# Channels dealt by parity: weight rows with one stride over 128 rows, and mu in two transfers

## The chip, the cores and the metric

The kernel runs on one core of a Trainium2 chip. The metric is the device time of one execution in microseconds, the median of several runs. The names of the engines: PE is TensorE (matmuls; PEld are its weight loads), DVE is VectorE, ACT is ScalarE, POOL is GpSimd. SP (SyncE) computes nothing here: it is the queue from which all transfers are issued, in program order. The transfers themselves are moved by 16 DMA engines.

## The reference

Two parts, one after the other: causal attention in blocks of 64 positions for 8 batches and 8 heads, then a channel mix on its output. All inputs are float32.

```python
# attention: q, k, v are [8, 8, 576, 64]
scores = np.matmul(q, k.transpose(0, 1, 3, 2)) / np.sqrt(64)
scores = np.where(block_i >= block_j, scores, -1e9)      # blocks of 64 positions
attn = softmax(scores)
x = np.matmul(attn, v)             # then [8, 576, 512]: 512 channels = 8 heads x 64

# channel mix: mu_k, mu_r [512], w_k [512, 1024], w_v [1024, 512], w_r [512, 512]
x_prev = x shifted by one position (zero first)
xk = mu_k * x + (1 - mu_k) * x_prev
xr = mu_r * x + (1 - mu_r) * x_prev
k = np.maximum(xk @ w_k, 0)
out = sigmoid(xr @ w_r) * ((k * k) @ w_v)
```

## The kernel before

The attention output is produced with channels on partitions, since the channel mix contracts over channels. For one batch, the heads are handled in two groups of four (Q = 0, 1). The 64 columns of V of a head are cut in two halves of 32, x = 0 and 1. A matmul with a 128x32 weight block of V fills 32 partitions, and the four heads g of the group fill the four 32-partition strips next to each other:

```python
R = D // 2                                   # 32

def products(ps, lhs, a, z, last):
    for kc in range((z + P - 1) // P):
        q0 = max(a, kc * P)
        for g in range(G):                   # G = 4 heads side by side
            nc.tensor.matmul(
                ps[g * R:g * R + R, q0 - a:z - a], lhs(kc, g),
                probs(b, 4 * Q + g, kc, q0, z - q0), ...,
                tile_position=(0, g * R))

def part(i):
    ...
    for x in range(2):
        products(PS[:, x * w:x * w + w],
                 lambda kc, g: VOs[b % 2][:, kc, 4 * Q + g,
                                          x * R:x * R + R],
                 a, z, True)
```

So block cc = 2 * Q + x of the 512 channels (128 channels on 128 partitions) holds, on partition 32 * g + r, channel 256 * Q + 64 * g + 32 * x + r. The rows of w_k and w_r, and mu_k and mu_r, have to be loaded in the same order. The rows of w_v follow the hidden units and are plain:

```python
def add_w(name, n, ranks, rank):
    src = {"k": moe_w_k, "r": moe_w_r, "v": moe_w_v}[name]
    if name == "v":
        src = src.rearrange("(cc p) (n j) -> n cc p j", p=P, j=C)
    else:
        src = src.rearrange("(q g s r) (n j) -> n q s g r j", g=G, s=2,
                            r=D // 2, j=C)
    for i in range(n):                       # 8 blocks of w_k, 4 of w_r, 8 of w_v
        ld = plan.buf("ld")
        ...
        t = load(("w", name, i), lambda: new("ld", [P, S], FP),
                 lambda d, cc=cc, half=half: [
                     (d[:, 0:C], src[half, cc] if name == "v" else
                      src[half, cc // 2, cc % 2])],
                 ranks[i], 0.8, takes=[ld])
        ...                                  # then a cast to fp16, on DVE, ACT or POOL

def mus():
    for dst, src in ((MUK, moe_mu_k), (MUR, moe_mu_r)):
        src = src.rearrange("(q g s r o) -> q s g r o", g=G, s=2, r=D // 2, o=1)
        for cc in range(CCn):                # CCn = 4
            nc.sync.dma_start(dst[:, cc:cc + 1], src[cc // 2, cc % 2])
```

Each block of weights is 128 rows of 512 float32, 256 KB. It goes to a buffer of the ring `ld` (10 buffers, shared with the loads of q and k) and is cast from there.

All the work is given as tasks to a small planner in the kernel's own code. It puts the tasks of every engine into one fixed order, from ranks and from assumed durations (0.8 us for a block of weights). On the chip each engine runs its list strictly in that order: a cast that waits for its block holds back everything behind it on its engine.

The normalization of the attention output on DVE (line 690) reads the products from PSUM and writes `xt`; the mixes (lines 740 and 752) make `xk` and `xr` from it. The channel mix's matmuls are at lines 788 (w_k), 821 (w_r) and 850 (w_v). Line 624 has the sums of the softmax, line 609 the products with V, line 539 the scores, line 561 the exponentials on ACT, line 569 zeros written on POOL behind them. Matmuls of `fill` (line 893) do no work for the result; they keep the PE busy in the beginning.

Of the kernel before, what the change touches and what calls it, by code (L numbers as in the profile page):

```python
# [175 lines left out]
def kernel(  # L176
# [12 lines left out]
    nc = tc.nc  # L189
    B, H, S, D = q.shape  # L190
    C = H * D
    DF = moe_w_k.shape[1]
    P = 128
    HP = H // 2
    CCn = C // P
    JCn = DF // P
    KP = S + D
    G = 4
# [21 lines left out]
    def new(ring, shape, dtype):  # L220
        return pools[ring].tile(shape, dtype, tag=ring, name="t_" + ring)
# [3 lines left out]
    VOs = [consts.tile([P, 5, H, D], F16, name=f"VO{i}") for i in range(2)]  # L225
# [26 lines left out]
    def step(b, n=0):  # L252
        return b * NP_ + n
# [4 lines left out]
    def load(dst_key, make, jobs, rank, dur, deps=(), takes=(), uses=()):  # L258
        def fn():
            if make is not None:  # L260
                tiles[dst_key] = make()
            for dst, src in jobs(tiles[dst_key]):
                nc.sync.dma_start(dst, src)
        return plan.add("SP", dur, rank, fn, deps, takes, uses)

    def on(eng, dur, rank, fn, deps, takes=(), uses=()):
        return plan.add(eng, dur, rank, fn, deps, takes, uses)

    def flex(key, alts, rank, fn, deps, takes=(), uses=()):


        eng = ENGINE.get(key, next(iter(alts)))
        t = plan.add(eng, alts[eng], rank, lambda: fn(eng), deps, takes, uses)
        t["key"], t["alts"] = key, alts
        return t

    def convert(eng, dst, src, scale=None):
        if eng == "ACT":
            if scale is None:
                nc.scalar.copy(dst, src)  # L280
            else:
                nc.scalar.activation(dst, src, AF.Copy, scale=scale)
            return
        e = nc.vector if eng == "DVE" else nc.gpsimd
        if scale is None:
            e.tensor_copy(dst, src)
        else:
            e.tensor_scalar_mul(dst, src, scale)
# [133 lines left out]
    def add_w(name, n, ranks, rank):  # L422
        src = {"k": moe_w_k, "r": moe_w_r, "v": moe_w_v}[name]
        if name == "v":
            src = src.rearrange("(cc p) (n j) -> n cc p j", p=P, j=C)
        else:
            src = src.rearrange("(q g s r) (n j) -> n q s g r j", g=G, s=2,
                                r=D // 2, j=C)
        for i in range(n):
            ld = plan.buf("ld")  # L430
            cc, half = (i % CCn, i // CCn) if name == "k" else (i, 0)
# [7 lines that stand above are left out]
            def fn(eng, i=i, cc=cc, half=half):  # L439
                dst = (WK[:, cc, half * C:half * C + C] if name == "k" else  # L440
                       WR[:, i] if name == "r" else WV[:, i])
                convert(eng, dst, tiles["w", name, i][:, 0:C],
                        0.5 if name == "v" else None)
            alts = {"POOL": 1.55 if name == "v" else 0.58, "DVE": 0.4,
                    "ACT": 0.53}
            usual = "POOL" if name == "k" else "ACT"
            cast["w", name, i] = flex(
                f"w{name}{i}", {usual: alts[usual], **alts}, rank, fn, [t],
                uses=[ld])
# [132 lines left out]
    def add_values(b, Q, ranks):  # L582
# [20 lines left out]
        R = D // 2  # L603
# [4 lines that stand above are left out]
                for g in range(G):  # L608
                    nc.tensor.matmul(  # L609
                        ps[g * R:g * R + R, q0 - a:z - a], lhs(kc, g),  # L610
                        probs(b, 4 * Q + g, kc, q0, z - q0),
                        start=(kc == 0 and last is not None),
                        stop=(kc == (z - 1) // P and last is not False),
                        tile_position=(0, g * R))
# [17 lines left out]
        def part(i):  # L632
            a, z = parts[i]
            PS = tiles["num", b, Q, i] = new(ring, [P, CH], FP)
            w = z - a
            for x in range(2):
                products(PS[:, x * w:x * w + w],
                         lambda kc, g: VOs[b % 2][:, kc, 4 * Q + g,
                                                  x * R:x * R + R],
                         a, z, True)  # L640

        def cost(i):
# [5 lines left out]
        for v, mine in enumerate(([0], [1, 2])):  # L648
# [3 lines left out]
            def fn(v=v, mine=mine):  # L652
                if v == 0:
                    sums()
                for i in mine:
                    part(i)
                if b == 0:
                    tiles["pa last"] = (tiles["num", b, Q, 2] if v else
                                        tiles["den", b, Q])
# [23 lines left out]
            for i, buf in zip(mine, bufs):  # L683
# [4 lines left out]
                def norm(i=i, a=a, z=z, c=c, at=at):  # L688
# [7 lines left out]
                n = on("DVE", 0.1 + (z - a) / 480, SOON, norm, [t, spr],  # L696
                       takes=[xtbuf[c]] if take else [],
                       uses=[buf, rd] + ([] if take else [xtbuf[c]]))
# [173 lines left out]

    def mus():
        for dst, src in ((MUK, moe_mu_k), (MUR, moe_mu_r)):
            src = src.rearrange("(q g s r o) -> q s g r o", g=G, s=2, r=D // 2,
                                o=1)
            for cc in range(CCn):
                nc.sync.dma_start(
                    dst[:, cc:cc + 1], src[cc // 2, cc % 2])

    def mu1():
        nc.vector.tensor_scalar_add(MUK1, MUK, -1.0)
# [3 lines left out]
    R = RANK  # L886
# [12 lines left out]
    at = {x: -99 + i for i, x in enumerate(R["loads"])}  # L899
    at |= R.get("at", {})  # L900
    t = on("SP", 0.6, at["mu"], mus, [])
    mu_ready.append(on("DVE", 0.3, at["mu"], mu1, [t]))
    for b in range(B):
        r = step(b)
# [17 lines left out]
        if b == 0:  # L922
            for name, n in (("k", 8), ("r", 4), ("v", 8)):
                add_w(name, n, [at[f"w{name}{i}"] for i in range(n)],
                      R["cast " + name])
# [71 lines left out]
```

## Time and profile before

The time is 310.37 us, the median of three runs (307.46 to 314.88). The profiled execution spans 308.1 us, with a mean granted PE clock of 0.939.

| engine | busy us | share of the span |
|---|---|---|
| PE | 263.6 | 86% |
| DVE | 213.4 | 69% |
| ACT | 186.6 | 61% |
| POOL | 125.3 | 41% |
| DMA queue of SP (16 engines) | | 72.9% |

In all, 51.43 MB are moved: 33.56 MB read from HBM and 9.44 MB written, and the transposes within the chip. The largest groups are ACT's 96 exponentials (96.0 us), the 288 matmuls with w_k (69.2 us) and the 296 with w_v (66.8 us).

In the profile, the span is cut into 40 slices; a digit is the busy share of an engine in that slice, in tenths (9 is 90% or more). Groups of instructions are named by line, engine, operation and what is written and read. A wait is put down to what ended it. A line of the order of time gives start and length in us, and in brackets the idle time before it and what ended that.

### The profile page before, as it was taken

What the parts mean: (1) busy time and instruction counts of PE and PEld (TensorE: products, weight loads), DVE (VectorE), ACT (ScalarE), POOL (GpSimd) and SP (SyncE); (2) the same over time, 40 slices, a digit from 0 to 9 for tenths busy, and PEclk for the clock granted to TensorE, in tenths of its full rate; (3) what the DMA queues carried; (4) which work ended last, traced back from release to release, by engine and by line L of the source; (5) the groups of instructions that cost most, each with busy time, mean ns of one, the idle gap of its engine ahead of it and who ended that gap; (6) DMA issues with size and microseconds to landing.
All of it is one profiled execution on the core that took longest, in us unless ns stands there. A gap on an engine that the chain in (4) does not pass through costs nothing. (4 is left out here: it accounts for less than half of the span.)

```text
span 308.1 us, 8562 instructions
## 1 busy us (share of the span) xinstructions
PE 263.6 (86%) x3460; PEld 139.6 (45%) x3460; DVE 213.4 (69%) x395; ACT 186.6 (61%) x268; POOL 125.3 (41%) x262
## 2 busy tenths in 40 slices
PE   8399832414979999879999999998999999997995
PEld 8287622202425444525454444453544544553443
DVE  1244513756399757868899996789499969997432
ACT  1058940344774898568759977974885795261440
POOL 2223342530273364043754833484582532370120
PEclk9789995955899999979999999999999999999999
DMA  5999527544998899999989999998989901201103
GB/s 113 265 263 258 131 68 173 148 129 126 178 219 182 209 226 203 215 256 161 207 198 232 192 203 255 224 180 223 223 176 199 222 3 65 75 2 68 68 15 123
DMA packets 137480, 51.43 MB, mean 167 GB/s; under 512 B 128096, under 2 KB 128352, under 8 KB 137440
## 3 DMA queue, kind: packets, MB, share of 16 engines
q1 hardware_dynamic: 137440, 50.88, 72.9%
q8 instruction: 27, 0.44, 0.6%
q14 instruction: 13, 0.11, 0.1%
HBM read 33.56 MB, written 9.44 MB: 140 GB/s over the span
## 5 line engine op out<-in xcount | busy, mean ns | idle before, releaser
L561 ACT ACTIVATE t_e<-t_s 128x1024 f16<-128x1024 f32 x96 | 96.0, 1025 | 28.1 <-PE t_s L539 27.0
L788 PE MATMUL t_mm<-t_xk,WK 128*128 128x512 f16 x288 | 69.2, 384 | 2.5 <-POOL t_xk L767 1.1
L850 PE MATMUL t_mm<-WV,t_k 128*128 128x512 f16 (+1 forms) x296 | 66.8, 374 | 1.1 <-DVE t_o L860 1.0
L569 POOL MEMSET t_e<- 64x128 f16 x128 | 24.4, 206 | 81.5 <-ACT t_e L561 78.6
L798 ACT ACTIVATE t_kr<-t_mm 128x512 f32<-128x512 f32 x72 | 42.4, 600 | 17.7 <-PE t_mm L788 14.0
L539 PE MATMUL t_s<-t_qkt 64*128 64x64 bf16 (+4 forms) x384 | 34.4, 285 | 12.4 <-ACT t_e L561 10.0
L850 PEld LDWEIGHTS <-t_k 128*128 128x128 f16 x296 | 27.9, 98 | 34.6 <-issue 3.6
L788 PEld LDWEIGHTS <-WK 128*128 128x128 f16 x288 | 26.3, 98 | 36.2 <-issue 9.2
L807 DVE TENSOR_TENSOR t_k<-t_kr 128x512 f16<-128x512 f32 x37 | 28.8, 789 | 19.2 <-ACT t_kr L798 19.0
L821 PE MATMUL t_mm<-WR,t_xr 128*128 128x512 f16 x144 | 38.1, 395 | 1.6 <-DVE t_o L860 1.2
L831 ACT ACTIVATE t_t<-t_mm 128x512 f32<-128x512 f32 x36 | 21.5, 600 | 27.4 <-PE t_mm L821 27.2
L807 POOL TENSOR_TENSOR t_k<-t_kr 128x512 f16<-128x512 f32 x24 | 27.9, 1172 | 23.1 <-ACT t_kr L798 22.6
L752 DVE SCALAR_TENSOR_TENSOR t_xk<-t_d,MUK,t_xt 128x512 f16<-128x512 f32 x36 | 33.2, 937 | 5.0 <-POOL t_d L740 4.4
L860 DVE SCALAR_TENSOR_TENSOR t_o<-t_t,t_mm 128x512 f32<-128x512 f32 (+1 forms) x37 | 24.7, 667 | 12.3 <-PE t_mm L850 8.5
L752 DVE SCALAR_TENSOR_TENSOR t_xr<-t_d,MUR,t_xt 128x512 f16<-128x512 f32 x36 | 30.7, 870 | 0.0
L740 POOL TENSOR_TENSOR t_d<-t_xt 128x512 f32<-128x512 f32 x16 | 20.5, 1284 | 20.6 <-DVE t_xt L690 12.0
L539 PEld LDWEIGHTS <-t_qkt 64*128 64x128 bf16 x384 | 13.0, 95 | 34.8 <-issue 27.9
L609 PEld LDWEIGHTS <-VO 128*32 128x32 f16 x1264 | 23.2, 98 | 5.6 <-issue 5.1
L893 PE MATMUL t_mm<-identb 128*128 128x128 bf16 x300 | 22.9, 236 | 2.2 <-POOL identb masks.py:199 1.4
L609 PE MATMUL t_m<-t_e,VO 128*32 128x192 f16 (+3 forms) x976 | 24.3, 242 | 0.0
L690 DVE TENSOR_TENSOR t_xt<-t_m,t_rd 128x384 f32<-128x384 f32 (+3 forms) x42 | 22.3, 549 | 2.0 <-PE t_m L609 1.6
L670 DVE RECIPROCAL t_c<-t_m 128x192 f32<-128x192 f32 x14 | 18.9, 1351 | 6.2 <-PE t_m L624 6.1
(58 smaller groups left out, 249.0 us busy)
## 6 DMA issues: line engine op xcount, KB each, us to landing
out_dram<-t_o SPq DMA_DIRECT2D x35, 256.0 KB
t_vl<-in_v_dram SPq DMA_DIRECT2D x32, 256.0 KB
t_ld<-in_q_dram SPq DMA_DIRECT2D x48, 128.0 KB
t_ld<-in_k_dram SPq DMA_DIRECT2D x48, 128.0 KB
t_ld<-in_q_dram SPq DMA_DIRECT2D x8, 288.0 KB
t_ld<-in_k_dram SPq DMA_DIRECT2D x8, 288.0 KB
t_ld<-in_moe_w_k_dram SPq DMA_DIRECT2D x8, 256.0 KB
t_ld<-in_moe_w_v_dram SPq DMA_DIRECT2D x8, 256.0 KB
```

The source lines that it names most:

```text
L539: nc.tensor.matmul(PS[:, h, col:col + n], qkt[rows, pr, 1, kc * P:kc * P + P], qkt[rows, pr, 0, q0:q0 + n], start=True, stop=True)
L561: nc.scalar.activation(tiles["e", b, pr][:, :, i, :], tiles["ps", b, it], AF.Exp, scale=ISQ)
L569: nc.gpsimd.memset(tiles["e", b, pr][D:P, :, i, z:z + D], 0.0)
L609: nc.tensor.matmul(ps[g * R:g * R + R, q0 - a:z - a], lhs(kc, g), probs(b, 4 * Q + g, kc, q0, z - q0), start=(kc == 0 and last is not None ...
L752: nc.vector.scalar_tensor_tensor(tiles[name, c][:, cc], tiles["d", c, cc], (MUK1, MUR1)[n][:, cc:cc + 1], tiles["xt", c][:, cc, 1:CH + 1], ...
L788: nc.tensor.matmul(ps, WK[:, cc, jc * P:(jc + 1) * P], tiles["xk", c][:, cc], start=(cc == 0), stop=(cc == CCn - 1))
L798: nc.scalar.activation(tiles["kr", c, jc], tiles["pk", c, jc], AF.Relu)
L807: (nc.vector if eng == "DVE" else nc.gpsimd).tensor_tensor(K2, KR, KR, ALU.mult)
L821: nc.tensor.matmul(ps, tiles["xr", c][:, cc, jt * P:(jt + 1) * P], WR[:, cc], start=(cc == 0), stop=(cc == CCn - 1))
L850: nc.tensor.matmul(ps[:, 0:w], tiles["k2", c][:, jc, jt * P:(jt + 1) * P], WV[:, jc, cols], start=(jc == 0), stop=(jc == JCn - 1))
L860: nc.vector.scalar_tensor_tensor(tiles["o", c, jt, part][:, 0:w], tiles["t", c, jt][:, cols], 1.0, tiles["pv", c, jt, part][:, 0:w], ALU.a ...
L893: nc.tensor.matmul(ps[:, 384:512], identb, identb, start=True, stop=True)
```

## The change

The 64 columns of a head are dealt to the two halves by parity, x = 0 the even and x = 1 the odd ones, where before they were cut into the first and the last 32. Partition 32 * g + r of block 2 * Q + x then holds channel 256 * Q + 64 * g + 2 * r + x. With p = 32 * g + r this is 256 * Q + 2 * p + x: one stride of two rows over all 128 partitions. So the source of a block of w_k or w_r is a pattern of 128 rows with one stride where it was 4 groups of 32 rows, and the four columns of a mu vector, which took four transfers, fit into one. In exchange the weight blocks of V are read with a stride of two elements. The purpose is simpler and fewer transfers at the start.

```diff
@@ add_w @@
-            src = src.rearrange("(q g s r) (n j) -> n q s g r j", g=G, s=2,
-                                r=D // 2, j=C)
+            src = src.rearrange("(q p s) (n j) -> n q s p j", p=P, s=2, j=C)
@@ part @@
-                         lambda kc, g: VOs[b % 2][:, kc, 4 * Q + g,
-                                                  x * R:x * R + R],
+                         lambda kc, g: VOs[b % 2][:, kc, 4 * Q + g, x:D:2],
@@ mus @@
-            src = src.rearrange("(q g s r o) -> q s g r o", g=G, s=2, r=D // 2,
-                                o=1)
-            for cc in range(CCn):
-                nc.sync.dma_start(
-                    dst[:, cc:cc + 1], src[cc // 2, cc % 2])
+            nc.sync.dma_start(dst[:, :].rearrange("p (q s) -> p q s", s=2),
+                              src.rearrange("(q p s) -> p q s", p=P, s=2))
```

## The prediction

> **What bounds the kernel now.** I read the page's forty slices first, then windows of the first 85 us, then what each engine waited for there, then the order of time of single engines around the longest wait. The page cuts the span into slices of 7.7 us:
>
> ```profile
> PE   8399832414979999879999999998999999997995
> ...
> DMA  5999527544998899999989999998989901201103
> GB/s 113 265 263 258 131 68 173 148 129 126 178 219 182 209 226 203 215 256 161 207 198 232 192 203 255 224 180 223 223 176 199 222 3 65 75 2 68 68 15 123
> ```
>
> From slice 11 (85 us) on the PE is full to the end: its waits after 85 us add up to 7.6 us, none over 1.2 us. So the last 223 us are a PE stream at its own pace. Before 85 us the PE does filler (the identity matmuls of `fill`, 22.9 us) or little at all: slices 6 to 10 read 3, 2, 4, 1, 4. The DMA is not full there either: 131, 68, 173, 148, 129, 126 GB/s after three slices at 260. What a change to these loads is worth is what it takes off the first 85 us.
>
> Two windows show what such a half-busy stretch is made of:
>
> ```profile
> core 0: us, PE busy (x) PEld busy (x) DVE busy (x) ACT busy (x) POOL busy (x), PEclk, DMA share, GB/s
> ...
> 54.80:56.80 2.00, 0.31 (x15) 0.28 (x14) 1.96 (x6) 1.59 (x2) 1.75 (x5) 0.85 0.26 94
> 63.00:67.00 4.00, 0.61 (x4) 0.28 (x4) 2.58 (x3) 2.16 (x3) 1.72 (x3) 0.50 0.27 96
> ```
>
> The busy share of the 16 DMA engines is 0.26 and 0.27, about four engines of sixteen, at 94 to 96 GB/s; in the best moment of the first 31 us the rate is 389 GB/s. The trace's raw completion records say the same: the 253 transfers raise their semaphores 3,828 times. If 233 rise 16 times and 20 only 5 times (four engines, and one rise for the absent twelve), that is 3,728 + 100 = 3,828, exactly. The twenty are the eight w_k loads, the four w_r loads and the eight transfers of mu. The w_v loads, just as large, belong to the 233.
>
> What waited before 85 us (engine and line, what ended the wait, us in total, times, longest):
>
> ```profile
> POOL WK L286 <- DMA t_ld<-in_moe_w_k_dram: 12.7, 4, 4.8
> ...
> DVE t_nl L286 <- DMA t_ld<-in_q_dram: 10.9, 2, 10.2
> PE t_mm L624 <- DVE t_xt L690: 10.7, 1, 10.7
> ...
> ACT WR L280 <- DMA t_ld<-in_moe_w_r_dram: 8.7, 3, 6.2
> ...
> DVE WR L286 <- DMA t_ld<-in_moe_w_r_dram: 5.6, 1, 5.6
> ```
>
> The PE's longest wait names DVE line 690. The issuing queue and DVE, in order of time (start, us, what; idle before and its releaser in brackets), show what stood in front of it:
>
> ```profile
> 34.03 5.74 SPq L878 DMA_DIRECT2D MUK<-in_moe_mu_k_dram  x4
> 39.81 3.19 SPq L878 DMA_DIRECT2D MUR<-in_moe_mu_r_dram  x4
> 43.09 0.53 SPq L263 DMA_DIRECT2D t_ld<-in_moe_w_r_dram  x1
> ```
>
> ```profile
> 50.62 0.43 DVE L286 CAST WR<-t_ld 128x512 f16<-128x512 f32 x1 [5.61 <-DMA t_ld<-in_moe_w_r_dram]
> 50.97 0.88 DVE L690 TENSOR_TENSOR t_xt<-t_mm,t_rd 128x512 f32<-128x512 f32 x2
> ```
>
> The eight issues of mu hold the queue from 34.0 to 43.0 us, each waiting for transfers ahead of it. Only then is the first w_r block issued, it lands at 50.6, DVE casts it, and the normalization that frees PSUM for the PE comes behind that cast, although its own inputs were there at about 41 us.
>
> **What the Trainium skill says.** "DMA: Bandwidth & Descriptors", section "Why a DMA increments its semaphore by 16 and not by 1": a transfer is spread over the largest number of engines up to 16 that divides the slowest dimension of both its access patterns. The source pattern of w_k, w_r and mu has g = 4 outermost, so four; w_v has 128 rows, so 16. The trace agrees (quarter share, 3,828 rises). The section "Rules for kernel authors" of the same page says to put a dimension that is a multiple of 16 outermost, which is what this change does. For the other side of the change, "SBUF — State Buffer", section "Door 1", says that two-byte elements can be read with strides of up to 8 elements at no cost; and "TensorE: Matmul & The Clock Gate", section "Weight-path perf modes", ties the fast weight load to 128 columns, so the 32-column loads of V have none to lose. No weight load of the kernel before is strided, so the trace is silent on these two.
>
> **The change, part by part.** The order of instructions on every engine is the same in both kernels, but for six DMA issues fewer. All durations and ranks of the planner are untouched.
>
> *Part 1, w_k and w_r over 16 engines.* Alone on four engines a block of 256 KB takes 262 kB / 96 GB/s = 2.7 us; twelve of them 33 us, with every other transfer's last quarter queued behind. At about 300 GB/s (my choice, between the 260 of the first full slices and the peak of 389) a block takes 0.9 us, so twelve take 11 us.
> - Start. Two w_k blocks go first and the first q lands behind them: DVE starts at 12.58, after a wait of 10.2 us. Two blocks and one q load of 295 kB are 0.82 MB, 2.7 us at 300 GB/s, after about 2 us to the first packets (the DMA rate over the first 31 us, in finer slices, starts so late): about 5.5 us with the landing, that is 7 us earlier. The bytes loaded before the first scores are a mix with 256-byte packets of v and ran near 260 GB/s already, so of the 7 us I keep 5.5 by the first exponentials (25.4 becomes about 20).
> - Middle, with part 2. The last transfers before mu are issued at 33.0, then at about 27.5. Two mu issues, estimated at 0.7 us each (the shortest before took 0.53 us), instead of 9.0 us put the w_r block at about 29.5. Loads issued at 85 to 90 us, with nothing ahead of them, land 3.0 us after their issue; with 3.5 us it is in at 33. DVE is free of earlier work at 39.3 − 5.5 = 33.8, casts, and can normalize once the PE has the products: 40.6 − 5.5 = 35.1, with releasing about 35.5. Before, this was 50.97: 15.5 us earlier, of which 10 are gained here.
> - Second half. From 51 to 75 us ACT, DVE and POOL cast eleven more blocks in program order, each as it comes: ACT stands 6.2, 2.8, 1.1, 1.4 and 0.25 us for w_r and w_v, DVE 5.3 us for a w_k block at 70.9, and the PE 7.4 us behind an exponential that stands behind ACT's w_r cast. Blocks that arrive 0.9 us apart are there before their casts. What is left is work: POOL has a subtraction of 1.5 us, a cast of 1.8 us and a q/k cast of 0.7 before the last b1 transposes, DVE then a reciprocal, shuffles, three normalizations, and 8 mixes of 0.75 to 1.5 us. By my estimate, adding those durations up, I get the last w_r mix at about 55 instead of 73.3, so the first w_r matmul at about 56 instead of 75.4: 19.5 us earlier in all, 4 of them gained here.
>
> *Part 2, mu.* 8 issues become 2; alone (without part 1) its share of the above would be some 6 to 7 us, of which the queue behind the four busy engines would eat a part.
>
> *Part 3, V with a stride of 2.* 1,264 weight loads of 97 ns (median), four of them side by side over column groups: 48 matmuls of the products take 1.07 us, 22 ns each. By the two pages nothing changes: 0 us. The weight load overlaps the matmuls of other column groups.
>
> *After 75 us.* No instruction of the PE stream gets slower, and everything it waits for starts earlier by about as much: the loads for batch 2 are issued from 64.9, right after the last weight block, and would go out at about 46. So the shift of the first w_r matmul reaches the end: 310.4 − 19.5 = 291.
>
> **Rivals.**
> - *Compute takes the place of the waits.* ACT's exponentials of 1.0 us, its casts and copies, and POOL's memsets behind them may fill 20 to 56 us in a less happy order than I see; then only the start and the middle count: 310.4 − 15.5 = 295. For it: POOL waits 24.2 us for ACT before 85 us. Against: before 85 us ACT is busy for about half of the time.
> - *The DMA becomes the bound of the steady part.* From 85 to 246 us its share is 1.00 at 210 GB/s. If the loads of batches 2 to 7 already set the pace, an earlier start of the PE stream runs into them. Against: the PE waits only 0.8 us for a transfer in that time, and the loads end at 246 us while the PE goes on to 308. And their start moves too. This would leave 12 to 15 us: 296 to 298.
> - *The strided weight loads cost.* If each took twice the 22 ns at which they now pass, 1,264 of them add 28 us, all on the full PE, and the kernel would lose: about 318. For it: nothing in the trace rules it out. Against: the two pages.
> - *More than I count.* The PE clock is 0.5 in most of 46 to 82 us because the PE is idle; with less idling it recovers sooner, and transfers may reach 389 GB/s: 285.
>
> **Range and chances.** The middle is 291. The first two rivals reach 298, the last 284, so 284 to 299 should hold it 8 times in 10. Faster by over 2% means below 304.2, a gain of 6 us, and the start alone brings nearly that: 0.91. Only the third rival makes it slower: 0.04. The rest, 0.05, is for partial losses.
>
> **What would show it.** Right: the first cast of q on DVE near 5.5 us instead of 12.6; slices 0 and 4 to 7 with the DMA rate near 200 to 300 GB/s and no plateau at 95; completion rises of 16 for all transfers; mu issued in under 2 us; the wait of PE line 624 for DVE line 690 gone; first w_r matmul near 56 us; the same 223 us or so from there to the end. Wrong: the plateau at 95 GB/s still there; weight loads of V above 97 ns, or the 48 products of one group longer than 1.07 us; new PE waits for transfers after the start; ACT or POOL full from 20 to 60 us.

## The result, and the profile after

The changed kernel takes 283.81 us (median of 4 runs, 281.99 to 286.41) against 310.94 us of the kernel before: a ratio of 0.914, with a 95% interval of 0.903 to 0.926. A second set of runs gave 282.89 us and 0.916 (0.908 to 0.923). The gain is 27 us; 19.5 were predicted, and 283.8 lies just under the low end of the range, 284.

The 40 slices of the page, now of 7.05 us each:

```profile
PE   8999856898999987999999999989999999997995
...
DMA  6999999794999899998999899999979103102113
GB/s 187 372 240 250 288 325 216 161 214 73 214 238 221 202 210 240 187 196 208 230 194 198 189 267 202 195 235 232 187 144 274 46 1 111 44 0 76 74 39 112
```

The stretch of slices that read 2, 4, 1 on the PE is gone, and the DMA is full from slice 1 to slice 6 (counted from 0). Its completions rise 3,952 times for 247 transfers, 16 each. The issuing queue and DVE, at the place that was shown of the kernel before:

```profile
28.01 0.42 SPq L873 DMA_DIRECT2D MUK<-in_moe_mu_k_dram  x1
28.49 0.46 SPq L873 DMA_DIRECT2D MUR<-in_moe_mu_r_dram  x1
29.05 0.42 SPq L263 DMA_DIRECT2D t_ld<-in_moe_w_r_dram  x1
```

```profile
34.15 0.83 DVE L286 CAST WR<-t_ld 128x512 f16<-128x512 f32 x1 [1.17 <-DMA t_ld<-in_moe_w_r_dram]
34.90 0.87 DVE L688 TENSOR_TENSOR t_xt<-t_mm,t_rd 128x512 f32<-128x512 f32 x2
```

mu holds the queue for 1.0 us where it held it for 9. The w_r block is issued at 29.05 instead of 43.09, and the normalization behind its cast comes at 34.90 instead of 50.97. The waits of the first 60 us:

```profile
DVE t_nl L286 <- DMA t_ld<-in_q_dram: 5.7, 3, 4.6
...
POOL WK L286 <- DMA t_ld<-in_moe_w_k_dram: 3.1, 2, 1.8
...
DVE WR L286 <- DMA t_ld<-in_moe_w_r_dram: 1.2, 1, 1.2
...
PE t_mm L623 <- DVE t_xt L688: 0.8, 1, 0.8
```

The same four read 10.9, 12.7, 5.6 and 10.7 us before, and ACT's wait for w_r (8.7 us) is no longer in the list. Where the difference sits is seen best from the first matmul with w_k. In order of time on the PE, first of the kernel before, then of the changed one:

```profile
75.41 4.69 PE L821 MATMUL t_mm<-WR,t_xr 128*128 128x512 f16 x12 [0.38 <-ACT WR L280]
...
81.85 4.76 PE L788 MATMUL t_mm<-t_xk,WK 128*128 128x512 f16 x20
```

```profile
48.40 1.03 PE L819 MATMUL t_mm<-WR,t_xr 128*128 128x512 f16 x2
50.17 4.45 PE L819 MATMUL t_mm<-WR,t_xr 128*128 128x512 f16 x10 [0.74 <-DVE t_xr L750]
...
57.11 4.49 PE L786 MATMUL t_mm<-t_xk,WK 128*128 128x512 f16 x20
```

The first w_r matmul waited for a cast of w_r; now the second group of them waits for a mix of DVE, which is work and not a transfer. And from the first w_k matmul to the end (window; length, busy us and number on PE, PEld, DVE, ACT, POOL, PE clock, DMA share, GB/s), before and after:

```profile
81.85:308.10 226.25, 215.05 (x2542) 102.94 (x2534) 179.27 (x324) 150.45 (x220) 100.95 (x204) 0.99 0.77 167
```

```profile
57.11:282.10 224.99, 214.76 (x2542) 102.94 (x2534) 180.88 (x324) 149.18 (x219) 99.85 (x203) 0.99 0.75 164
```

226.25 and 224.99 us, with the same work in them. Of the 26.0 us between the two spans, 24.7 are gained before the first w_k matmul.

### The profile page after: what moved, and what is told of

It reads as the page before. It is cut to its first block, busy times and chain, and to the rows that moved or that the text cites. A ratio compares the mean times of both kernels' runs of the same rounds, so it can differ in the third digit from the quotient of the medians.

```text
span 282.1 us, 8552 instructions
## 1 busy us (share of the span) xinstructions
PE 261.7 (93%) x3460; PEld 137.7 (49%) x3460; DVE 215.1 (76%) x395; ACT 186.3 (66%) x268; POOL 125.1 (44%) x262
## 5 line engine op out<-in xcount | busy, mean ns | idle before, releaser
L819 PE MATMUL t_mm<-WR,t_xr 128*128 128x512 f16 x144 | 38.9, 401 | 1.9 <-DVE t_o L858 1.2
L858 DVE SCALAR_TENSOR_TENSOR t_o<-t_t,t_mm 128x512 f32<-128x512 f32 (+1 forms) x37 | 24.7, 666 | 12.0 <-PE t_mm L848 7.1
L688 DVE TENSOR_TENSOR t_xt<-t_m,t_rd 128x384 f32<-128x384 f32 (+3 forms) x42 | 22.2, 549 | 5.3 <-PE t_m L608 5.2
L608 PE MATMUL t_m<-t_e,VO 128*32 128x192 f16 (+3 forms) x976 | 24.6, 243 | 0.0
L888 PE MATMUL t_mm<-identb 128*128 128x128 bf16 x300 | 21.9, 230 | 2.2 <-POOL identb masks.py:199 1.4
L819 PEld LDWEIGHTS <-t_xr 128*128 128x128 f16 x144 | 13.3, 101 | 20.7 <-issue 6.6
```

Of the source, the lines that this page charges most:

```text
L608: nc.tensor.matmul(ps[g * R:g * R + R, q0 - a:z - a], lhs(kc, g), probs(b, 4 * Q + g, kc, q0, z - q0), start=(kc == 0 and last is not None ...
L688: nc.vector.tensor_tensor(xt_tile(c)[:, 2 * Q:2 * Q + 2, 1 + at:1 + at + w], tiles["num", b, Q, i][:, 0:2 * w].rearrange("p (s t) -> p s t ...
L819: nc.tensor.matmul(ps, tiles["xr", c][:, cc, jt * P:(jt + 1) * P], WR[:, cc], start=(cc == 0), stop=(cc == CCn - 1))
L858: nc.vector.scalar_tensor_tensor(tiles["o", c, jt, part][:, 0:w], tiles["t", c, jt][:, cols], 1.0, tiles["pv", c, jt, part][:, 0:w], ALU.a ...
```

## The experiments

Two theories from the start: *engines* (w_k and w_r blocks on 4 of the 16 DMA engines were the loss), and *mu* (nine us of issue queue in the middle were). Later the first is made sharper: what counts is the busiest engine's bytes. Times are medians; ratios are to the kernel before in the same set of runs (311.41, 308.73 and 309.64 us in the three sets), with 95% intervals. A ratio can differ from the quotient of the two medians by up to 0.5%. Where rows and channels don't match, the kernel does the same work on rows paired otherwise than in the reference.

**Weights alone.** On the kernel before:

```diff
-            src = src.rearrange("(q g s r) (n j) -> n q s g r j", g=G, s=2,
-                                r=D // 2, j=C)
+            src = src.rearrange("(q p s) (n j) -> n q s p j", p=P, s=2, j=C)
```

> The kernel before with the new source pattern of w_k and w_r alone; mu stays in eight transfers and V in halves, so rows and columns no longer match and only the time is of use. Theory 'engines' (the w_k and w_r blocks ran on 4 of 16 DMA engines, and that was most of it): 285 to 290 us, because the eight mu issues, with free engines ahead of them, take about 0.5 us each and cost at most 3 to 4 us of the queue. Rival 'mu' (nine us of queue in the middle were most of it): 298 us or more.

288.36 us, ratio 0.921 (0.913 to 0.930): 23.0 of the 27 us by the medians, 24.6 by the ratio, as the theory *engines* has it. The eight mu issues took 5.3 us here instead of 8.9, though still on four engines (3,960 completion rises: 245 × 16 + 8 × 5).

**mu alone.** On the kernel before:

```diff
-            src = src.rearrange("(q g s r o) -> q s g r o", g=G, s=2, r=D // 2,
-                                o=1)
-            for cc in range(CCn):
-                nc.sync.dma_start(
-                    dst[:, cc:cc + 1], src[cc // 2, cc % 2])
+            nc.sync.dma_start(dst[:, :].rearrange("p (q s) -> p q s", s=2),
+                              src.rearrange("(q p s) -> p q s", p=P, s=2))
```

> The kernel before with the two mu transfers alone; the order of mu then doesn't match the channels, so only the time is of use. Theory 'engines': the queue gains some us at 34 us, but the w_r block behind it still goes through four busy engines: 303 to 308 us. Rival 'mu': 297 us or less. If the two parts simply add, this gain and that of the weights alone sum to the 27 us of the whole.

305.55 us, ratio 0.980 (0.974 to 0.987): 5.9 us. The two parts alone sum to 28.9 us and nearly add up to the whole. The rival *mu* has fallen.

**V without the stride.** On the changed kernel:

```diff
-                         lambda kc, g: VOs[b % 2][:, kc, 4 * Q + g, x:D:2],
+                         lambda kc, g: VOs[b % 2][:, kc, 4 * Q + g,
+                                                  x * R:x * R + R],
```

> The changed kernel with the weight blocks of V read without a stride again (halves instead of parity; channels then don't match the weight rows, so only the time is of use). Theory 'the stride is free': within 0.5% of the changed kernel, 283 to 285 us, V weight loads at 98 ns and 48 products in 1.07 us in both. Rival 'the stride costs': faster than the changed kernel by 2 us or more.

282.86 us, ratio 0.908 (0.901 to 0.914), against 283.81 and 282.89 of the changed kernel in two other sets (0.914 and 0.916, intervals that overlap). The groups of weight loads (busy us, mean ns of one), with the stride and then without:

```profile
L608 PEld LDWEIGHTS <-VO 128*32 128x32 f16 x1264 | 23.3, 98 | 5.8 <-issue 5.3
```

```profile
L608 PEld LDWEIGHTS <-VO 128*32 128x32 f16 x1264 | 23.4, 99 | 5.5 <-issue 5.1
```

The same loads in the same time. A full group of 48 products, with the stride and then without:

```profile
32.95 1.07 PE L608 MATMUL t_mm<-t_e,VO 128*32 128x256 f16 x48
```

```profile
33.74 1.07 PE L608 MATMUL t_mm<-t_e,VO 128*32 128x256 f16 x48
```

Single groups take longer, the longest of them 1.90 us: one in the second profile of the changed kernel, but also one in the run with the weights alone, which reads V without a stride. So these are no sign against the stride, which costs nothing that these runs can tell.

**The old row pattern on 16 engines.** Is it the number of engines or the plain row pattern? On the kernel before, complete:

```diff
                      lambda d, cc=cc, half=half: [
-                         (d[:, 0:C], src[half, cc] if name == "v" else
-                          src[half, cc // 2, cc % 2])],
+                         (d[:, 0:C], src[half, cc])] if name == "v" else [
+                         (d[32 * g:32 * g + 32, 0:C],
+                          src[half, cc // 2, cc % 2, g]) for g in range(G)],
```

> The kernel before, complete, with each block of w_k and w_r in four transfers of 32 rows, one for each g; pattern of rows, bytes, mu and V as before. Theory 'engines': each quarter has 32 rows outermost and so runs on 16 engines; the 36 more issues of about 0.4 us cost the queue up to 14 us, partly hidden: 286 to 298 us, and no plateau at 95 GB/s. Rival 'the single stride itself' (a plain row pattern is what makes the transfers fast, whatever the number of engines): 308 us or more.

297.32 us, ratio 0.950 (0.942 to 0.958). Same rows, same bytes, four times as many transfers, and 14 us faster: the number of engines is the cause, not the single stride. The completions agree: 4,535 rises, where 281 transfers on 16 engines and the eight of mu on four make 4,536. What is missing to 284 is at least in part the queue: a w_k block of four transfers holds it for 2.0 us (0.5 us a piece), mu still takes 4.7 us, and the first w_r block is issued at 40.05 instead of 29.05.

**mu in eight transfers, on 16 engines.** On the changed kernel, complete, beside a second run of the changed kernel itself:

```diff
-            nc.sync.dma_start(dst[:, :].rearrange("p (q s) -> p q s", s=2),
-                              src.rearrange("(q p s) -> p q s", p=P, s=2))
+            src = src.rearrange("(q p s o) -> q s p o", p=P, s=2, o=1)
+            for cc in range(CCn):
+                nc.sync.dma_start(
+                    dst[:, cc:cc + 1], src[cc // 2, cc % 2])
```

> The changed kernel once more, as the base for the three runs beside it: 282 to 286 us.

> The changed kernel, complete, with mu in eight transfers of one column each (128 rows outermost) instead of two. Theory 'few us of queue': eight issues of about 0.5 us instead of two delay the first w_r block by 3 us, and part of it is absorbed before the first w_k matmul: 1 to 3 us over the changed kernel. Rival 'mu counts for the 6 us it gained in the kernel before': 5 us or more over it.

282.89 us for the changed kernel and 286.29 (ratio 0.927, 0.920 to 0.934) with eight transfers: 3.4 us. The w_r block is issued at 32.96 instead of 29.05, and its cast on DVE starts at 35.63 instead of 34.15. This is a little more than I expected and well under the rival's 5 us: in the kernel before, mu's gain of 5.9 us came in part from its place behind the busy engines.

**Eight engines, and two.** On the changed kernel, only the rows of w_k and w_r taken in 8 (or 2) groups:

```diff
-            src = src.rearrange("(q p s) (n j) -> n q s p j", p=P, s=2, j=C)
+            src = src.rearrange("(q g s r) (n j) -> n q s g r j", g=8, s=2,
+                                r=16, j=C)        # and g=2, r=64
```

> The changed kernel with the w_k and w_r rows taken in 8 groups of 16 (rows then don't match the channels; only the time is of use), so each of these blocks runs on 8 engines; bytes, number of transfers, mu and V as in the changed kernel. Theory 'the busiest engine sets the first part': until the last weight block 12.3 MB are loaded, 3.1 MB of them w_k and w_r; the busiest engine carries 0.58 + 3.1/16 = 0.77 MB with sixteen, 0.97 with eight, 1.36 with four. Between four and sixteen the first w_k matmul moved by some 20 us (76.8 with the two mu transfers alone, 57.1 now), so a third of that for eight: 6 to 8 us, 290 to 292 us. Rival 'only a block's own duration counts' (2.7 us alone on four engines, 1.3 on eight, and anything under the 1.5 us or so between two casts is hidden): 283 to 286 us.

> The same with 2 groups of 64 rows, so on 2 engines. Theory 'the busiest engine': 0.58 + 3.1/2 = 2.15 MB against 0.77, and 20 us for 0.59 MB between sixteen and four: 47 us over the changed kernel, about 330 us (320 to 345), with a plateau near 48 GB/s. Rival (beyond four engines the loads run beside other work of the first part): 310 to 315 us.

289.64 us with eight (ratio 0.937, 0.928 to 0.946), 329.74 with two (1.068, 1.055 to 1.081), where 290 to 292 and about 330 were expected. The first w_k matmul in each, eight and then two:

```profile
62.55 4.49 PE L787 MATMUL t_mm<-t_xk,WK 128*128 128x512 f16 x20
```

```profile
102.74 4.50 PE L787 MATMUL t_mm<-t_xk,WK 128*128 128x512 f16 x20
```

And the slices of the kernel with two engines (8.2 us each):

```profile
DMA  3699444232139989999997989999898930200203
GB/s 101 199 273 233 119 126 113 81 105 78 65 102 198 174 197 239 212 217 249 215 166 197 231 186 203 251 198 201 228 220 180 223 99 3 99 34 17 112 2 128
```

The thin stretch is back and longer, down to 65 GB/s in slice 10 (counted from 0). It is not the 48 that two engines would give alone, since other transfers run beside them. From the first w_k matmul to the end it is 225.5 and 225.2 us in the two spans of 288.1 and 327.9: all of the loss lies ahead of it. Against the changed kernel the busiest engine carries 0.20 MB more with eight and 1.38 MB more with two; 6.75 and 46.85 us for that are 34 us per MB both times. An engine alone needs 2.7 us for the quarter of a block (65.5 kB), 41 us per MB; so, by this estimate, about four fifths of what the busiest engine is held up reaches the end in these runs, and no threshold is seen at which the loads hide. Four engines fit in: in the run with mu alone the first w_k matmul comes at 76.82, 19.7 us later than in the changed kernel, for 0.59 MB more. That is 33 us per MB; by the same measure it is 28 with eight engines and 33 with two.

**q ahead of the w_k blocks, in both kernels.** The list of loads begins with the four names of q instead of `wk2`, `wk7`; in one run mu and the first w_r block also move ahead of `wv2`:

```diff
- 'loads': ['wk2', 'wk7', 'g0q', 'b1g1q', 'b1g0q', 'g1q', 'g0k', 'b1v0',
+ 'loads': ['g0q', 'b1g1q', 'b1g0q', 'g1q', 'wk2', 'wk7', 'g0k', 'b1v0',
```

> The kernel before, complete, with the eight q loads ahead of the two w_k blocks and all else as it was (weights on four engines). My prediction counted 5.5 us for the start, because q stood behind two slow blocks. If that queueing is a loss of its own, moving q ahead gains 4 to 6 us: 303 to 306 us. By the theory 'busiest engine' the four engines have the same bytes to carry, and the first w_k matmul stays near 82 us: 308 to 312 us, although the first cast of q comes 6 to 8 us earlier.

307.43 us, ratio 0.989 (0.982 to 0.996). It gains 2.2 us by the medians and 3.4 by the ratio, between the two expectations; with runs from 303.7 to 312.6 the size is loose. Of this kernel, first on DVE, then on the PE:

```profile
3.73 1.45 DVE L286 CAST t_nl<-t_ld 128x576 bf16<-128x576 f32 x2 [1.34 <-DMA t_ld<-in_q_dram]
```

```profile
78.97 4.64 PE L788 MATMUL t_mm<-t_xk,WK 128*128 128x512 f16 x20
```

q arrives 8.9 us earlier, and the first w_k matmul comes 2.9 us earlier. That is 2.9 of the 24.7 us which the change brings there. What the four engines have to carry in all is not changed by who goes first, and that sum decides most of it.

> The changed kernel, complete, with the eight q loads issued ahead of the two w_k blocks (two names moved in the list of loads; the planner then also moves a few casts and copies of the first 40 us). Theory 'sum of bytes over sixteen engines' (the first part is set by all that has to be loaded and by DVE and ACT behind it): the first cast of q comes 2 us earlier, but the first w_k matmul doesn't: 282 to 285 us. Rival 'whoever stands first in the queue matters': the 2 us reach the end, 280 to 281 us.

> The same with mu and the first w_r block issued before the third w_v block as well. In the changed kernel DVE waited 1.2 us for that w_r block; with it there, the chain from the normalization on may start up to 1 us earlier: 281 to 284 us if the first part still hangs on that block, the same as the run without it if not.

285.25 us, ratio 0.924 (0.918 to 0.929), and 283.61, ratio 0.916 (0.914 to 0.918). Neither is faster than the changed kernel with its 283.81 and 282.89. In the profiled run of the first, w_k matmuls began at 54.17 and the span was 279.9 us, so there may be something in it, but the other runs of the set, up to 287.4, don't bear it out. With w_r there early (its cast on DVE at 28.18), the first w_k matmul of the second came at 56.27 against 57.11 and 56.42: no gain from having that block early is seen. The total doesn't decide between the two expectations: 283.61 lies within the 281 to 284 us of the first, and is 1.6 us under the run without it, which scatters by 6.

## Why the prediction was right, and what it missed

- *What bounds the kernel.* Right. In ten of the thirteen profiles the time from the first w_k matmul to the end is 225.0 to 226.3 us, however long the first part took (54 to 103 us). The other three are told of at the end.
- *Four engines for w_k, w_r and mu.* Right; the runs with 8 and 2 engines and the one with the old pattern in quarters settle it. The rule of the Trainium skill ("DMA: Bandwidth & Descriptors", section "Why a DMA increments its semaphore by 16 and not by 1") gave the number of engines each time the outermost dimension was varied: with 8 groups the 247 transfers should rise 235 × 16 + 12 × 9 = 3,868 times, with 2 groups 235 × 16 + 12 × 3 = 3,796, and the traces hold exactly so many.
- *Start.* The first q cast came at 7.0 us, not 5.5, but the first exponentials at 19.2, not 20. Right in size. The raw completion records show what stood in the way. Of the first q load in the kernel before, twelve engines were done between 6.68 and 7.21 us and the last four between 12.32 and 12.55, behind the two w_k blocks; in the changed kernel all 16 were done between 4.96 and 7.00. But q's place in the queue is only half of it: moving q ahead in the kernel before brought the first exponentials from 25.4 to 22.2, and the rest came only with the weights on 16 engines.
- *Middle.* w_r issued at 29.05 (29.5 predicted), landed at 34.1 (33), normalization at 34.9 (35.5). Right.
- *Second half.* This is the term that was mis-sized. I put the last w_r mix at 55 us and the first w_r matmul at 56; the mix ended at 50.1, from 73.3 before, and the matmul came at 48.4. The last mix, first before and then after:

```profile
72.56 0.75 DVE L752 SCALAR_TENSOR_TENSOR t_xr<-t_d,MUR,t_xt 128x512 f16<-128x512 f32 x1
```

```profile
49.23 0.88 DVE L750 SCALAR_TENSOR_TENSOR t_xr<-t_d,MUR,t_xt 128x512 f16<-128x512 f32 x1
```

Relative to the normalization's gain of 16.1 us the second half brought 7 more, where I had 3. I had added POOL's subtraction and casts (4.0 us) and DVE's reciprocal, normalizations and mixes one after the other. They ran side by side: from the normalization at 34.90 to the end of the last mix DVE was idle for only 0.9 us, and its reciprocal began while POOL still had its q/k cast to do:

```profile
38.99 1.34 DVE L668 RECIPROCAL t_c<-t_mm 128x192 f32<-128x192 f32 x1
```

```profile
39.73 0.66 POOL L286 CAST t_nl<-t_ld 128x576 bf16<-128x576 f32 x1
```

By the spans 26.0 us were gained where I had 19.5. Of the 6.5 us between, this is 4.3. The middle brought 0.6 more than I had, and the stretch from the last mix to the first w_k matmul 0.4 (8.5 us before, 7.0 after, of which I had counted 1.1). The last part gives 1.3, which is no more than the ten profiles scatter there.

- *mu.* 6 to 7 us were given for it alone, less a part eaten by the queue behind it: 5.9 us measured. I had the eight issues waiting for the transfers ahead of them. With the weights on 16 engines they still took 5.3 of the 8.9 us: 3.6 us went with the busy engines, the rest did not.
- *V with a stride.* 0 us predicted, 0 within the scatter.
- *Rivals.* Compute did not take the place of the waits at 15.5 us. The loads of the steady part did not stop the shift: in that part the PE still waits for a transfer only once, 1.1 us. The strided weight loads cost nothing. "More than I count", 285, was the nearest in number, but not for its reason: most of what I had not counted is the work of DVE and POOL side by side. The mean PE clock did rise, from 0.939 to 0.975; what that alone was worth, these runs don't show.

## What to carry to other kernels

When the DMA share of a stretch sits at about a quarter, look at the outermost dimension of the transfers in it: here a pattern of 4 groups of 32 rows ran on four engines, and the q load behind two of them ended with those four, 5 us after the other twelve. Then add up the bytes of the busiest engine, not of the transfers: its load, more than who stands first in the queue, set the time. It can pay to permute channels through a whole computation only to make one row pattern plain, where the permutation costs nothing elsewhere, as the strided weight loads here.

## What was not expected of the hardware

In three of the thirteen profiles (weights alone, mu alone, and q ahead in the kernel before) the part from the first w_k matmul to the end took 229 to 232 us. All three have the same event, and no other profile has it: one of POOL's seven corrections of 4 columns of xk, 0.21 us at the median and at most 0.65 us in the other profiles, takes 2.19 us. In the kernel with the weights alone, on POOL and then on the PE:

```profile
138.67 2.19 POOL L766 TENSOR_TENSOR t_xk<-t_xt,MUK 128x4 f16<-128x4 f32 x1 [1.07 <-DVE t_xk L751]
```

```profile
140.91 3.57 PE L787 MATMUL t_mm<-t_xk,WK 128*128 128x512 f16 x8 [3.01 <-POOL t_xk L766]
```

```profile
139.00:143.00 4.00, 2.09 (x6) 0.69 (x6) 1.78 (x4) 0.79 (x2) 2.92 (x6) 0.64 0.66 180
143.00:147.00 4.00, 4.00 (x66) 2.28 (x66) 1.70 (x2) 2.20 (x4) 0.00 (x0) 0.51 0.47 105
147.00:151.00 4.00, 4.00 (x82) 2.17 (x78) 3.89 (x11) 3.72 (x6) 2.03 (x5) 1.00 0.79 165
```

The PE idles for 3.0 us, and from 143 us its clock is granted at 0.51 for four (the number after the five busy times in the windows). With q ahead in the kernel before it is the same: idle for 3.0 us, then a clock of 0.50. With mu alone the PE idles for 3.0 us too, but its clock stays at 1.00. The last part is 3.5 us longer there, and 5 to 6 us in the other two, than the 225.7 us or so of the ten: so much goes with one correction of 4 columns.

The cause stays open. POOL's instruction ends at 140.86, just after two mixes of DVE from 139.39 to 140.79. "SBUF — State Buffer" of the Trainium skill, section "Who interferes with whom", says that a DVE instruction with two inputs in SBUF contends with a POOL instruction that reads there, and such are these two. But in the run with eight engines DVE's cast and the same two mixes start 0.38 and 0.74 us after the correction, against 0.38 and 0.72 here, and it takes 0.21 us. So the mixes beside it are not enough to explain it. Each of the three profiles is of the slowest of its kernel's four runs; whether the event is part of why runs of one kernel scatter by 1 to 2% is not shown.
